# Scaling decoded weights by rms_g: GpSimd's multiplication given to ScalarE in a fused attention and MLP kernel

## The chip, the cores and the metric

The kernel runs on one core of a Trainium2 chip. The metric is the device time of one execution in microseconds. The core's engines are TensorE (PE in the profile: matmuls; PEld: their weight loads), VectorE (DVE), ScalarE (ACT), GpSimd (POOL) and SyncE (SP, which issues the DMAs). Each engine takes its instructions in the order in which the code issues them; a semaphore makes an instruction wait for one of another engine.

## What is computed

Linear attention with random features, then a gated MLP with RMS normalization, then a second MLP. Inputs are 64-bit floats. After the attention, x has 2304 tokens and 512 features:

```python
def _moe_ref(x, w_gate, w_val, w_out, rms_g):       # d_ff = 1536
    rms = np.sqrt(np.mean(x * x, axis=-1, keepdims=True) + 1e-06)
    xn = x / rms * rms_g
    g = xn @ w_gate
    silu = g * (1.0 / (1.0 + np.exp(-g)))
    val = xn @ w_val
    return (silu * val @ w_out).astype(np.float32)

def _moe2_ref(x, w_in, w_out):                      # d_ff = 2048
    h = x @ w_in
    g = h * (1.0 / (1.0 + np.exp(-h)))
    return (g @ w_out).astype(np.float32)
```

The factor rms_g belongs to a row of w_gate and of w_val, so the kernel multiplies the weights by it and leaves x alone.

## The kernel before

**Precision.** Every product of the two MLPs is made from split operands: a high part (a copy rounded to fp32r) and a low part (value minus high part), in three matmuls (PASS: high by high, high by low, low by high).

**Tokens and sweeps.** The tokens lie in five blocks j: four of 512 tokens and block 4 of 256. The hidden columns lie in groups f of 128; five sweeps cover the 12 groups of the gated MLP (2, 3, 2, 3, 2 groups) and six sweeps the 16 of the second. A sweep goes over all blocks. For each group of a block in the gated MLP (g1_glu), TensorE makes the gate product (12 matmuls, PSUM tile "ps_g", of which there are four), ScalarE takes its SiLU (line 259), TensorE makes the value product, VectorE multiplies both (line 265), ScalarE copies the high part of the result (line 235) and VectorE subtracts the low part (line 236). The product with w_out of the whole block, here called the second product (g2_glu, line 296), is held back: it is issued behind the first gate product of the next block, and in block 4 behind the first pair of products. VectorE adds its four tiles ("ps_y", four too) into ya (line 307); in the first sweep ScalarE copies them (line 305).

**Weights.** A weight block is a job: a gate (g), value (v) or w_out (o) block, named below with its group, as v4 or o4. The jobs go through a pipeline with one stage per tick:

- load: a DMA of 512 KB into raw;
- decode (w_decode): five steps on VectorE (lines 156 to 167), two integer additions on GpSimd (line 170), and for g and v blocks a multiplication by rms_g on GpSimd (line 173). All write one tile m, of which there are two;
- w_high: ScalarE copies the high part (line 186);
- w_low, called w_lo here: VectorE subtracts the low part (line 189), which reads m too.

In one tick the oldest job comes first: w_low of one, w_high of the next, decode of a third, load of a fourth. stream() yields the cost of each product just ahead of issuing it (and of each second-product tile just behind it); the loop at the end of the kernel adds these costs and calls a tick where they pass 3.2 us (while the weights of the second sweep are not all there) or 5.5 us. A product whose weights are missing (prep.need) calls ticks too. The place of a tick's instructions in each engine's order follows from these sums alone.

**The first phase** (to about 200 us) holds the attention and the first sweep of blocks 0 to 2. A planner (run_order) orders it; there add_weight issues the same steps for 9 jobs, seven of them g or v blocks (four of the first sweep, then g2, v2 and g3), with w_decode's step 7 for the multiplication. The other 17 g and v blocks (v3, g4, v4, then g5 to v6, g7 to v9, g10 to v11) go through the ticks.

Of the kernel before, what the change touches and what calls it, by code (L numbers as in the profile page):

```python
# [8 lines left out]
F32 = mybir.dt.float32  # L9
# [4 lines left out]
AF = mybir.ActivationFunctionType  # L14
# [6 lines left out]
def kernel(  # L21
# [14 lines left out]
    nc = tc.nc  # L36
# [7 lines left out]
    KC = DM // P  # L44
    TB = 4
    EDGE, SHIFT = 72, 16
    scale = 1.0 / float(D) ** 0.25
# [42 lines left out]
    g_sb = const.tile([P, KC], F32)  # L90
# [17 lines left out]
    f = 0  # L108
# [4 lines left out]
    f = 0  # L113
# [26 lines left out]
    def w_load(job, st, n):  # L140
        raw = rawp.tile([P, KC, P, 2], U32, tag=f"raw{n}", name=f"raw{n}", bufs=1)
        ap = job[3]
        if len(ap.shape) == 2:
            nc.sync.dma_start(out=raw.rearrange("p c f w -> p (c f w)"), in_=ap)
        else:
            nc.sync.dma_start(out=raw.rearrange("p c f w -> p c (f w)"), in_=ap)
        words = raw.rearrange("p c f w -> p (c f) w")
        st.low, st.high = words[:, :, 0], words[:, :, 1]


    def w_decode(job, st, step, n=None):
        ts, tt = nc.vector.tensor_scalar, nc.gpsimd.tensor_tensor
        low, high = st.low, st.high
        if step == 0:
            st.m = rawp.tile([P, KC * P], U32, tag=f"m{n}", name=f"m{n}", bufs=1)
            ts(out=st.m, in0=high, scalar1=1, scalar2=1,  # L156
               op0=ALU.logical_shift_left, op1=ALU.logical_shift_right)
        elif step == 1:
            ts(out=low, in0=low, scalar1=2.0 ** -29, scalar2=None, op0=ALU.mult)
        elif step == 2:  # L160
            mf = st.m.bitcast(F32)
            ts(out=mf, in0=mf, scalar1=EXP_LO, scalar2=EXP_HI, op0=ALU.max, op1=ALU.min)
        elif step == 3:
            ts(out=high, in0=high, scalar1=0x80000000, scalar2=0x40000000,
               op0=ALU.bitwise_and, op1=ALU.bitwise_or)
        elif step == 4:
            ts(out=st.m, in0=st.m, scalar1=3, scalar2=None, op0=ALU.logical_shift_left)
        elif step < 7:
            mi = st.m.bitcast(I32)
            tt(out=mi, in0=mi, in1=(low if step == 5 else high).bitcast(I32), op=ALU.add)  # L170
        else:
            mf = st.m.bitcast(F32).rearrange("p (c f) -> p c f", c=KC)
            tt(out=mf, in0=mf, in1=g_sb.rearrange("p (c o) -> p c o", o=1).to_broadcast([P, KC, P]), op=ALU.mult)

    def scaled(job):
        return job[2][1] in "gv"

# [16 lines left out]
    class Prep:  # L194
# [13 lines left out]
        def tick(self):  # L208
            for e in self.pipe:
                job, st, n, step = e  # L210
                if step == 0:
                    for s in range(8 if scaled(job) else 7):
                        w_decode(job, st, s, n)
                else:
                    (w_high if step == 1 else w_low)(job, st)
                e[3] += 1
            self.pipe = [e for e in self.pipe if e[3] < 3]
            if self.jobs:
                self.n ^= 1
                e = [self.jobs.pop(0), State(), self.n, 0]  # L220
                w_load(e[0], e[1], self.n)
                self.pipe.append(e)
# [679 lines left out]
    def add_weight(job, n, gate):  # L902
        st = State()
        pr = W_PRIO + n

        def load(o):
            w_load(job, st, o.slot["raw"])

        lop = Op("ld_w", "SP", 2.0, load, gate, pr, ["raw"])
        prev = head = None  # L910
        for s in range(5):
            prev = Op(
                "w_dec", "DVE", 0.37, lambda o, s=s: w_decode(job, st, s, o.slot.get("wm")), [lop, prev], pr,
                [] if s else ["wm"], port=True,
            )
            head = head or prev
        for s in (5, 6, 7) if scaled(job) else (5, 6):
            prev = Op(
                "w_add", "Pool", 1.38, lambda o, s=s: w_decode(job, st, s), [prev, g_op], pr,
                free=[(lop, "raw")] if s == 6 else [],  # L920
            )
        hi = Op("w_hi", "ACT", 0.54, lambda o: w_high(job, st), [prev], pr)
        w_done[job[2]] = Op("w_lo", "DVE", 0.61, lambda o: w_low(job, st), [hi], pr, free=[(head, "wm")], port=True)
# [98 lines left out]
    with tc.manual_schedule():  # L1022
# [16 lines left out]
        def split_omega(e, c):  # L1039
# [3 lines left out]
            else:  # L1043
# [8 lines left out]
                out=om, in_=omega.rearrange("m (o d) -> m o d", o=1).to_broadcast([P, 2, D])  # L1052
# [67 lines left out]
```

## Time and profile before

| | |
|---|---|
| median of 3 runs | 998.92 us (998.87 to 999.29) |
| the profiled execution | 998.12 us, span from first to last instruction 996.0 us |
| granted TensorE clock, mean | 0.999 |
| busy: PE, DVE, ACT, POOL | 979.2, 575.9, 381.0, 312.7 us |
| multiplications by rms_g on GpSimd | 24, from 46.5 to 451.6 us |

A row of the timeline gives start and duration in us, engine, line, operation, the tile written and the tiles read, sizes, and a count where neighbours are merged. Square brackets hold the time the engine stood idle just before and what ended it. An engine that is seldom busy can still be in the way, if another waits for it at the wrong time; so the places where TensorE is not busy are looked for first, and then what ended them.

### The profile page before, as it was taken

To read this page: it belongs to the slowest core of one execution; us is meant where nothing else is said; L and a number is where in the kernel's file an instruction comes from. 1 tells how busy PE (TensorE), PEld (TensorE's weight loads), DVE (VectorE), ACT (ScalarE), POOL (GpSimd) and SP (SyncE) were. 2 spreads that over 40 slices of the span, in tenths; PEclk is the share of its full clock that TensorE was granted. 3 is DMA by queue.
4 is the path that set the end of the run, shared out by engine and by line. 5 is a ranking of instruction groups with operands and counts; after the bars stand their busy time and mean duration, and the time that the engine had idled before them with its cause. 6 is when DMAs were issued, how large, how long until landed. Compare 5 with 4: busy or idle time off the path is not lost.

```text
span 996.0 us, 15344 instructions
## 1 busy us (share of the span) xinstructions
PE 979.2 (98%) x5999; PEld 835.1 (84%) x5999; DVE 575.9 (58%) x1167; ACT 381.0 (38%) x855; POOL 312.7 (31%) x325
## 2 busy tenths in 40 slices
PE   7998999999999999999999999999999999999998
PEld 6988998888788888888888888888888888888887
DVE  6999998358843346685234683623644644525633
ACT  5999996543221112212112334442322322222321
POOL 7877764236610025453000332312312312201200
PEclk9999999999999999999999999999999999999999
DMA  7554312003210002222000220110200211100023
GB/s 197 148 128 108 106 45 64 22 23 105 85 43 1 1 22 64 80 80 74 1 1 1 64 64 23 62 43 22 85 22 22 68 39 27 59 1 22 21 85 106
DMA packets 69112, 55.58 MB, mean 56 GB/s; under 512 B 26160, under 2 KB 63280, under 8 KB 69040
## 3 DMA queue, kind: packets, MB, share of 16 engines
q1 hardware_dynamic: 69040, 54.60, 18.4%
q8 instruction: 47, 0.77, 0.3%
q14 instruction: 25, 0.20, 0.1%
HBM read 49.87 MB, written 4.72 MB: 55 GB/s over the span
## 4 chain that ended last, share of the span: by engine, by line
PE 89%; DVE 5%; ACT 3%; issue 1%; DMA 0%; SPq 0%; DVEq 0%; ACTq 0%
PE g L242 44%; PE y L329 20%; PE y L296 12%; PE b L626 4%; PE b L242 3%; PE b L999 2%; ACT e L668 2%; PE kv L694 1%; PE b L752 1%; PE b L777 1%; DVE small L643 1%; PE b L605 1%; DVE w L189 1%; PE b L878 1%; DVE m L156 1%
## 5 line engine op out<-in xcount | busy, mean ns | idle before, releaser
L242 PE MATMUL g<-xs,w 128*128 128x512 f32 (+1 forms) x2256 | 468.0, 366 | 0.0
L242 PEld LDWEIGHTS g<-xs,w 128*128 128x128 f32 x2256 | 391.1, 188 | 70.0
L170 POOL TENSOR_TENSOR m<-m,raw 128x512 int32<-128x512 int32 x136 | 190.5, 1401 | 562.3 <-issue 421.4
L236 DVE TENSOR_TENSOR h<-s,h 128x512 fp32r<-128x512 f32 (+1 forms) x134 | 96.9, 724 | 185.1 <-ACT h L235 185.1
L329 PE MATMUL y<-w,h 128*128 128x512 f32 (+1 forms) x870 | 200.8, 388 | 0.0
L329 PEld LDWEIGHTS y<-w,h 128*128 128x128 f32 x870 | 162.2, 188 | 33.2
L235 ACT ACTIVATE h<-s 128x512 fp32r<-128x512 f32 (+1 forms) x134 | 78.7, 588 | 183.3 <-DVE s L265 161.3
L296 PE MATMUL y<-h,w 128*128 128x512 f32 (+1 forms) x648 | 136.0, 366 | 1.3 <-DVE w L189 1.2
L296 PEld LDWEIGHTS y<-h,w 128*128 128x128 f32 x648 | 112.0, 189 | 22.0 <-DVE w L189 1.8
L276 ACT ACTIVATE s<-g 128x512 f32<-128x512 f32 (+1 forms) x80 | 44.4, 556 | 171.0 <-PE g L242 170.9
L340 DVE TENSOR_TENSOR ya<-y,ya 128x512 f32<-128x512 f32 (+1 forms) x91 | 62.1, 684 | 57.9 <-PE y L329 56.6
L186 ACT ACTIVATE w<-m 128x512 fp32r<-128x512 f32 x68 | 42.9, 631 | 116.4 <-POOL m L170 69.0
L307 DVE TENSOR_TENSOR ya<-y,ya 128x512 f32<-128x512 f32 (+1 forms) x80 | 50.1, 634 | 53.5 <-PE y L296 53.3
L668 ACT ACTIVATE e<-b,nb 128x128 f32<-128x128 f32 x272 | 78.5, 418 | 4.7 <-DVE nb L656 4.0
L265 DVE TENSOR_TENSOR s<-s,g 128x512 f32<-128x512 f32 (+1 forms) x54 | 33.8, 626 | 76.8 <-PE g L242 75.1
L626 PE MATMUL b<-bd,hl 128*128 128x256 f32 x432 | 65.2, 295 | 2.8 <-DVE hl L614 1.8
L626 PEld LDWEIGHTS b<-bd,hl 128*128 128x128 f32 x432 | 56.3, 193 | 5.9 <-DVE hl L614 2.5
L189 DVE TENSOR_TENSOR w<-m,w 128x512 fp32r<-128x512 f32 x68 | 55.6, 817 | 0.2 <-ACT w L186 0.2
L643 DVE TENSOR_REDUCE small<-b 128x4 f32<-128x512 f32 x72 | 50.0, 695 | 5.2 <-PE b L626 2.5
L259 ACT ACTIVATE s<-g 128x512 f32<-128x512 f32 (+1 forms) x54 | 29.5, 547 | 59.2 <-PE g L242 59.1
L558 POOL TENSOR_TENSOR sq<-sq 128x256 f32<-128x256 f32 (+2 forms) x80 | 45.0, 579 | 1.9
L554 POOL TENSOR_TENSOR sq<-x 128x512 f32<-128x512 f32 (+1 forms) x40 | 39.0, 982 | 19.1 <-DVE small L649 9.9
(69 smaller groups left out, 737.8 us busy)
## 6 DMA issues: line engine op xcount, KB each, us to landing
raw<-in_moe_w_out_dram SPq DMA_DIRECT2D x28, 512.0 KB, 3.5
raw<-in_moe_w_in_dram SPq DMA_DIRECT2D x16, 512.0 KB, 3.6
raw<-in_moe_w_gate_dram SPq DMA_DIRECT2D x12, 512.0 KB, 3.6
raw<-in_moe_w_val_dram SPq DMA_DIRECT2D x12, 512.0 KB, 3.5
x<-in_k_dram SPq DMA_DIRECT2D x16, 256.0 KB, 3.2
va<-in_v_dram SPq DMA_DIRECT2D x32, 128.0 KB, 3.2
x<-in_q_dram SPq DMA_DIRECT2D x16, 256.0 KB, 2.9
out_dram<-ya SPq DMA_DIRECT2D x15, 256.0 KB, 2.0
```

The costliest lines, as they stand in the source:

```text
L170: tt(out=mi, in0=mi, in1=(low if step == 5 else high).bitcast(I32), op=ALU.add)
L189: nc.vector.tensor_tensor(out=st.t[:, 1, :], in0=st.m.bitcast(F32), in1=st.t[:, 0, :].bitcast(F32), op=ALU.subtract)
L235: nc.scalar.activation(out=ht[:, 0, :], in_=s, func=AF.Copy)
L236: nc.vector.tensor_tensor(out=ht[:, 1, :], in0=s, in1=ht[:, 0, :].bitcast(F32), op=ALU.subtract)
L242: nc.tensor.matmul(out=ps, lhsT=w[:, a, cc * P:(cc + 1) * P], rhs=xs[j][:, c, cc, :], start=(n == 0), stop=(n == 3 * KC - 1),)
L296: nc.tensor.matmul(out=ps, lhsT=wt[1, "o", f][:, a, d * P:(d + 1) * P], rhs=hs[f][:, c, :], start=(n == 0), stop=(n == nn - 1),)
L307: nc.vector.tensor_tensor(out=y[:, d, :], in0=ps, in1=y[:, d, :], op=ALU.add)
L329: nc.tensor.matmul(out=ps, lhsT=hs[f][:, a, t * P:(t + 1) * P], rhs=wt[2, "p", f][:, c, d0:d1], start=(n == 0), stop=(n == nn - 1),)
L340: nc.vector.tensor_tensor(out=o[:, t, d0:d1], in0=ps, in1=o[:, t, d0:d1], op=ALU.add)
L626: nc.tensor.matmul(out=st.ps[r][:, 2 * j:2 * j + 2, :].rearrange("p h m -> p (h m)"), lhsT=st.hl[:, c, 2 * r + j, :], rhs=bd[:, a, :], sta ...
L643: nc.vector.tensor_reduce(out=st.mx[:, G * r:G * r + G], in_=st.ps[r], axis=AX.X, op=ALU.max)
L668: nc.scalar.activation(out=st.e[r][:, h, :], in_=st.ps[r][:, h, :], func=AF.Exp, bias=st.nb[:, G * r + h:G * r + h + 1],)
```

## The change

In the ticks the decode stage now issues steps 0 to 6 only. For g and v blocks it then issues w_scale: four ScalarE operations, each of which multiplies 128 columns of m in place (the 128 rows of the weight block that share one column of g_sb) by an operand per partition. They stand in ScalarE's order behind w_high of the job before and ahead of whatever the stream issues next. The first phase is left as it was.

```diff
+    def w_scale(st):
+        mf = st.m.bitcast(F32).rearrange("p (c f) -> p c f", c=KC)
+        for c in range(KC):
+            nc.scalar.activation(out=mf[:, c], in_=mf[:, c], func=AF.Copy, scale=g_sb[:, c:c + 1])
...
             for e in self.pipe:
                 job, st, n, step = e
                 if step == 0:
-                    for s in range(8 if scaled(job) else 7):
+                    for s in range(7):
                         w_decode(job, st, s, n)
+                    if scaled(job):
+                        w_scale(st)
                 else:
                     (w_high if step == 1 else w_low)(job, st)
```

## Rows read from the trace of the kernel before

**Rows 1.** The page, part 1: busy us, share of the span, instructions.
```profile
PE 979.2 (98%) x5999; PEld 835.1 (84%) x5999; DVE 575.9 (58%) x1167; ACT 381.0 (38%) x855; POOL 312.7 (31%) x325
```

**Rows 2.** Windows: busy us of each engine in two stretches of 50 us.
```profile
200.00:250.00 50.00, 49.03 (x251) 41.20 (x249) 35.80 (x56) 19.49 (x36) 23.88 (x18) 1.00 0.20 64
...
300.00:350.00 50.00, 50.00 (x274) 43.52 (x273) 15.16 (x26) 7.33 (x14) 0.00 (x0) 1.00 0.00 1
```

**Rows 3.** The chain that ended last: start, us, engine, tile, line, count.
```profile
212.24 1.68 issue
...
248.53 1.78 DVE w L189
250.35 6.64 PE y L296 x28
...
354.21 5.44 PE y L296 x24
```

**Rows 4.** Three lines by themselves: ns of one (min/median/max), first and last start.
```profile
L173 POOL TENSOR_TENSOR m<-m,g_sb x24: 1036/1077/1470, 46.5 to 451.6; 128x512 f32<-128x512 f32 x24
...
L668 ACT ACTIVATE e<-b,nb x272: 359/403/567, 14.2 to 160.3; 128x128 f32<-128x128 f32 x136
...
L189 DVE TENSOR_TENSOR w<-m,w x68: 678/684/1804, 63.4 to 946.6; 128x512 fp32r<-128x512 f32 x68
```

**Rows 5.** Timeline from 212 to 229 us.
```profile
212.31 2.70 POOL L170 TENSOR_TENSOR m<-m,raw 128x512 int32<-128x512 int32 x2 [12.48 <-DVE m L167]
...
217.66 0.43 DVE L236 TENSOR_TENSOR h<-s,h 128x256 fp32r<-128x256 f32 x1 [0.48 <-ACT h L235]
...
223.19 1.26 DVE L162 TENSOR_SCALAR m<-m 128x512 f32<-128x512 f32 x1
...
224.71 0.42 DVE L167 TENSOR_SCALAR m<-m 128x512 uint32<-128x512 uint32 x1
224.74 0.37 ACT L259 ACTIVATE s<-g 128x256 f32<-128x256 f32 x1
...
226.04 0.80 DVE L236 TENSOR_TENSOR h<-s,h 128x256 fp32r<-128x256 f32 x1 [0.49 <-ACT h L235]
...
227.56 3.04 PE L296 MATMUL y<-h,w 128*128 128x256 f32 x24
...
228.59 1.15 DVE L156 TENSOR_SCALAR m<-raw 128x512 uint32<-128x512 uint32 x1
```

**Rows 6.** Timeline of ScalarE in the first phase.
```profile
143.55 1.14 ACT L668 ACTIVATE e<-b,nb 128x128 f32<-128x128 f32 x4
144.55 0.41 ACT L610 ACTIVATE hl<-b 128x256 fp32r<-128x256 f32 x1
```

**Rows 7.** Timeline from 362 to 368 us, around weight g7.
```profile
362.19 2.69 POOL L170 TENSOR_TENSOR m<-m,raw 128x512 int32<-128x512 int32 x2 [80.88 <-issue]
...
367.92 0.69 DVE L265 TENSOR_TENSOR s<-s,g 128x512 f32<-128x512 f32 x1 [2.50 <-PE g L242]
```

**Rows 8.** Timeline from 246 to 248 us, around weight g5.
```profile
246.19 0.42 DVE L167 TENSOR_SCALAR m<-m 128x512 uint32<-128x512 uint32 x1
...
247.23 0.63 ACT L235 ACTIVATE h<-s 128x512 fp32r<-128x512 f32 x1 [2.31 <-DVE s L265]
```

**Rows 9.** Timeline from 403 to 415 us, around weight v9.
```profile
403.27 0.43 DVE L156 TENSOR_SCALAR m<-raw 128x512 uint32<-128x512 uint32 x1
...
404.62 0.42 DVE L167 TENSOR_SCALAR m<-m 128x512 uint32<-128x512 uint32 x1
...
406.69 1.87 DVE L307 TENSOR_TENSOR ya<-y,ya 128x512 f32<-128x512 f32 x3
...
412.70 0.91 DVE L236 TENSOR_TENSOR h<-s,h 128x256 fp32r<-128x256 f32 x1 [0.48 <-ACT h L235]
...
414.18 3.04 PE L296 MATMUL y<-h,w 128*128 128x256 f32 x24
```

**Rows 10.** Timeline from 430 to 442 us, around weight g10.
```profile
430.48 2.69 POOL L170 TENSOR_TENSOR m<-m,raw 128x512 int32<-128x512 int32 x2 [3.09 <-issue]
...
433.40 8.46 PE L296 MATMUL y<-h,w 128*128 128x512 f32 x36
```

## The prediction

> **What bounds the kernel now.** First the busy times: TensorE is busy for 98% of the span, no other engine for more than 58% [rows 1]. Then the stretches, for where its idle time lies: 0.97 us of 50 between 200 and 250 us, none between 300 and 350 [rows 2]. So behind the first phase there is next to nothing to win, and what makes TensorE wait shows in full. Then the chain that ended last: it leaves TensorE for VectorE between 212 and 250 us, where the low halves of the decoded weights are written, and comes back at 250.35, when VectorE's w_lo of block 4 of w_out lets a product go on; from there it is TensorE alone, 24 matmuls of 512 columns in 5.44 us [rows 3], 0.227 each, and half of that for the 256 columns of token block 4. The stretch to 250 is the one place where VectorE's order counts.
>
> **What goes.** 17 of the 24 multiplications on GpSimd [rows 4]; seven weights are prepared in the first phase and keep it. At some 1.1 us that is 19 us of an engine that is busy 31% [rows 1]. Nobody on TensorE's path waits for it, save by way of VectorE, whose operations lose time beside GpSimd's: a decode step of 0.42 took 1.26 where a multiplication ran, another 1.15 [rows 5].
>
> **What comes.** 17 times four ScalarE operations, no DMA and no queue of DMAs moved. Their own price is not in the trace. The nearest are the four exponentials of 128 columns, with an operand per row as here: the next operation started 1.00 us after the first [rows 6]. Above, four of their median duration of 0.403 [rows 4] with no overlap are 1.6 us; below 1.00 nothing speaks for a gain, as ScalarE did none of this. I take 1.1, close to the like shape. By the Trainium skill (ScalarE: Activation LUTs, What ACT_TABLE_LOAD costs) such an operation takes about 0.39 us and overlaps the next by 0.09: an estimate of 1.17 for four, 0.4 us more in the sum below. The row is shorter than that.
>
> **What moves is a wait.** Before, ScalarE met a weight first in w_high, one tick after the decode. Now it stands at the first scaling until VectorE's five steps and GpSimd's two additions (2.70 us [rows 5]) of the same tick are done. Queued behind it is whatever the code issues next. Walking through the yields of the stream and adding their amounts, behind the 17 stand: the high copy of an activation 8 times, a SiLU 4, the next w_high 4, a copy out of PSUM once. Behind a held SiLU or high copy, VectorE in turn stands at the product or the low half. TensorE has four PSUM tiles to run ahead with, so it stops only where the low half of a block's last column group comes too late for the second product; that follows one first product later.
>
> Where it is hidden: for g7 the additions end at 364.88, the scaling at 366.0, so high copy and low half end by 367.4, ahead of VectorE's next product at 367.92 [rows 7]. Nothing lost, and g8, g9, v7, v8 go like it: their lateness is below 0.7 us, with a whole first product to make it good. If that cover went, each would cost about what the next cases do. Three places are not hidden.
>
> (A) Weight v4, next in ScalarE's queue the SiLU of the 256-column block. v3 first: its additions end at 215.01, so the high copy behind it starts at 216.15. That copy (0.63 as in [rows 8]), its low half (0.7), and product, copy and low half of the following short block (1.3) bring VectorE to 218.8, where it was at 218.09 [rows 5]. g4's scaling only holds back copies out of PSUM whose tiles nobody wants yet. This 0.7 comes back, since a step of v4's decode no longer lies beside a multiplication (1.26 against 0.42): the decode ends at 225.1 as before. Additions to 227.85, scaling to 228.95. SiLU to low half took 1.30 to its start, and 0.43 where nothing disturbed it [rows 5]: done at 230.7. The second product starts at 227.56 and wants that low half four matmuls of 0.113 later, at 228.0. **TensorE waits 2.7.**
>
> (B) The same for VectorE: its low half ends at 230.7 instead of 226.84, 3.9 late. Its next w_lo then meets no GpSimd (0.68, the median of [rows 4], where there were 1.75 up to the step at 228.59; less 1.1), and that step no multiplication (0.42 instead of 1.15; less 0.7) [rows 5]: 2.1 late. VectorE is full to 250, so that stays. g5's decode, ended at 246.61 [rows 8], ends at 248.7; additions 251.5; scaling 252.6; then the high copy of block 4, which ran from 247.23 [rows 8], to 253.3, its low half 0.7 to 254.0, w_lo 0.7 to 254.7. TensorE went on at 250.30 behind that w_lo [rows 3]. **The delay is now 4.4, A included.** The three weights after it (v5, g6, v6) hold ScalarE too, but behind them stands a second product of 8 us that needs nothing of it; by the same steps v6 lets ScalarE go at about 270, and the next second product starts at about 277.
>
> (C) Weight v9, again with the short block's SiLU behind it. Its decode ended at 405.04 [rows 9]; lateness from g9 adds 0.2. Additions to 408.05, scaling to 409.15, SiLU to low half to 410.9. Behind these on VectorE stand four additions into ya (0.62 each, to 413.4), a w_lo (0.7 [rows 4]) and the decode of the next weight (1.77 from first start to last end), to 415.7, and then the product, the copy and the low half of the second column group, this last beside GpSimd (0.91 [rows 9]): 417.5. The second product started at 414.18 [rows 9] and wants it at 414.6. **2.9 lost.**
>
> (D) Weight g10, with the high copy of block 9 behind it. Additions end at 433.17, scaling 434.3, high copy 434.9, low half 435.65, w_lo 436.3. The second product starts at 433.40 [rows 10] and wants the last of these after 8 matmuls, at 435.2. **1.1 lost.**
>
> Sum: 4.4 + 2.9 + 1.1 = 8.4. The profiled execution took 998.12, its span 996.0; this becomes 1006.5. The median of the runs is 998.92, 0.8 above the profiled one, so the forecast is 1007.3.
>
> Bounds. The scaling enters A twice (v3 and v4), B once more, C twice, D once. At 1.0 the sum is 0.6 less, at 1.6 it is 3 more: 1010.3. If v3's lateness does not come through (0.7 in A), C's low half finds GpSimd quiet (0.5) and D is hidden (1.1), the forecast is 1005.0; with the lower price 1004.4.
>
> **Rivals.** *The cover holds.* The low halves come in time, ScalarE's wait is slack everywhere, and the time stays at about 998.9. For it: ScalarE is busy for 19.49 of 50 us there [rows 2], and g7 shows the cover. Against: at v4 the second product wants the low half at 228.0, 1.2 us after it was done [rows 5], and the hold of ScalarE, from 225 to 229, is longer. That is the point that decides: holds that delay a low half by less than 1.2 us cost nothing. It is the outcome on the other side.
>
> *VectorE freed.* Between 212 and 228 a multiplication cost VectorE about 0.8 and 0.7 us [rows 5], and TensorE waited for VectorE at 250. If only that counted, the 0.97 of idle up to 250 [rows 2] and the 0.35 from there to 250.35 [rows 3] would go: 997.6 at best, which is still within 0.2%. The Trainium skill says why such operations suffer (SBUF — State Buffer, SBUF: two separate sides): GpSimd and VectorE take a shared port by turns, each for a whole instruction. The trace agrees: w_lo has a median of 0.684 and a maximum of 1.804 [rows 4]. Against it as the outcome: the hold of ScalarE is longer than what VectorE gains.
>
> *Not what it says.* Were the scalings put next to w_high in the queue, nobody would wait, and the time is 998.9. But the rows of before stand in the order in which the code issues them.
>
> *Part of it.* B's chain finds slack or C's second column group passes early: A by itself (2.7) up to A with C (5.6), 1001.6 to 1004.5.
>
> *More.* The scalings run one after another because they read and write the same tile, with a gap each: 2.4 for four, 8 more in the sum, 1011 to 1015.
>
> **How the numbers follow.** Forecast 0.70; cover holds 0.05; VectorE freed 0.03; not what it says 0.02; part of it 0.10; more 0.10. Range 1004.0 to 1011.5, which leaves out the rivals; with edges of *more* and *part of it* that fall inside it holds near 0.8. This kernel's time can be told from no change beyond about 0.2%, 2.0 us. Faster by that much needs more idle time of TensorE than there is: 0.02. Within it: cover, VectorE freed and misplacement, less that 0.02: 0.08. Slower: 0.90.
>
> **What would show it.** GpSimd: 7 multiplications left, 68 ScalarE operations at the new line. ScalarE's longest waits are for GpSimd's additions at that line. TensorE waits for low halves at three places: about 2.7 near 228, near 255 some 1.7 more than the kernel before had at 250, some 3 near 420, 1 near 443. Wrong if TensorE idles at other second products (then the cover of g7 to v8 or of v6 was misjudged), or if the four scalings are far from 1.1.

## The result and the profile after

The changed kernel takes 1008.92 us (median of 4 runs, 1007.35 to 1009.31), the kernel before 998.89 (4 runs). The ratio is 1.0099, with a 95% interval of 1.0084 to 1.0114: 10.0 us slower, where 8.4 were forecast. The profiled execution took 1007.35 us with a span of 1005.5, 9.2 and 9.5 above those of before.

The page of the changed kernel, parts 1 and 5 (its lines from 174 on stand 5 lower, from 217 on 7 lower: line 296 is now 303, 242 is 249, 235 and 236 are 242 and 243, 189 is 194; the scaling is line 178):

```profile
PE 982.6 (98%) x5999; PEld 836.0 (83%) x5999; DVE 561.6 (56%) x1167; ACT 400.3 (40%) x923; POOL 290.8 (29%) x308
...
L303 PE MATMUL y<-h,w 128*128 128x512 f32 (+1 forms) x648 | 139.6, 370 | 7.4 <-ACT h L242 6.1
...
L178 ACT ACTIVATE m<-m,g_sb 128x128 f32<-128x128 f32 x68 | 21.8, 391 | 74.1 <-POOL m L170 74.1
```

Beside [rows 1], GpSimd lost 17 operations and 22 us, VectorE 14 us with the same number of operations, and ScalarE gained 68 operations and 19 us. None of that is near a limit. What counts is idle time: 7.4 us of TensorE ahead of the second product (1.3 before), mostly for ScalarE's high copy of an activation, and 74.1 us of ScalarE ahead of the scaling, for GpSimd's additions. The view of waits gives the same pairs (total us, times, longest):

```profile
ACT m L178 <- POOL m L170: 74.1, 17, 10.0
...
PE y L303 <- ACT h L242: 6.1, 3, 2.2
PE y L303 <- DVE h L243: 1.0, 3, 0.5
```

Seventeen holds of ScalarE, and four places where TensorE runs dry. The idle times in brackets add up to less than the loss, so losses are taken below from the start of one product to the start of a later one. The first place, the timeline from 224 to 231 us, to be read against [rows 5]:

```profile
224.43 0.41 DVE L167 TENSOR_SCALAR m<-m 128x512 uint32<-128x512 uint32 x1
...
224.98 2.69 POOL L170 TENSOR_TENSOR m<-m,raw 128x512 int32<-128x512 int32 x2 [1.43 <-ACT m L178]
...
227.70 1.28 ACT L178 ACTIVATE m<-m,g_sb 128x128 f32<-128x128 f32 x4 [0.87 <-POOL m L170]
227.72 0.51 PE L303 MATMUL y<-h,w 128*128 128x256 f32 x3
228.89 0.36 ACT L266 ACTIVATE s<-g 128x256 f32<-128x256 f32 x1
229.28 0.42 DVE L272 TENSOR_TENSOR s<-s,g 128x256 f32<-128x256 f32 x1 [4.44 <-ACT s L266]
...
230.18 0.43 DVE L243 TENSOR_TENSOR h<-s,h 128x256 fp32r<-128x256 f32 x1 [0.48 <-ACT h L242]
230.20 3.11 PE L303 MATMUL y<-h,w 128*128 128x256 f32 x21 [1.97 <-ACT h L242]
```

The SiLU of the short block, at 224.74 before, starts at 228.89, right behind the four scalings. VectorE stands 4.44 us for it. TensorE does three matmuls of the second product at 227.72 and then stands until the high copy is there. The second place, from 248 to 262 us; first TensorE in the kernel before (see also [rows 8]), then the changed kernel:

```profile
250.35 6.64 PE L296 MATMUL y<-h,w 128*128 128x512 f32 x28 [1.20 <-DVE w L189]
256.83 5.38 PE L242 MATMUL g<-xs,w 128*128 128x512 f32 x23
```

```profile
248.12 0.42 DVE L167 TENSOR_SCALAR m<-m 128x512 uint32<-128x512 uint32 x1
...
248.67 2.67 POOL L170 TENSOR_TENSOR m<-m,raw 128x512 int32<-128x512 int32 x2 [2.48 <-issue]
...
251.38 1.28 ACT L178 ACTIVATE m<-m,g_sb 128x128 f32<-128x128 f32 x4 [4.53 <-POOL m L170]
252.56 0.61 ACT L242 ACTIVATE h<-s 128x512 fp32r<-128x512 f32 x1
...
253.23 0.49 PE L303 MATMUL y<-h,w 128*128 128x512 f32 x1 [2.21 <-ACT h L242]
...
253.82 0.68 DVE L194 TENSOR_TENSOR w<-m,w 128x512 fp32r<-128x512 f32 x1
253.96 8.46 PE L303 MATMUL y<-h,w 128*128 128x512 f32 x29 [0.23 <-DVE h L243]
...
262.26 13.08 PE L249 MATMUL g<-xs,w 128*128 128x512 f32 x57
```

w_lo ends at 254.50, 4.2 us behind the 250.30 of before. But the 29 matmuls from 253.96 on take 8.46 us, where 28 took 6.64 before. The windows say why. A row has the length of the window, the busy us and the instructions of PE, PEld, DVE, ACT and POOL, and at its end the granted clock as a share of full speed, the DMA share and GB/s:

```profile
250.00:252.00 2.00, 1.02 (x5) 0.52 (x3) 0.00 (x0) 0.62 (x3) 1.29 (x1) 1.00 0.00 0
252.00:254.00 2.00, 0.54 (x2) 0.23 (x2) 0.79 (x2) 2.00 (x6) 0.00 (x0) 0.94 0.77 214
254.00:256.00 2.00, 2.00 (x4) 1.41 (x5) 1.97 (x6) 0.18 (x1) 0.00 (x0) 0.50 0.17 57
256.00:258.00 2.00, 2.00 (x8) 1.63 (x7) 0.91 (x2) 0.00 (x0) 1.48 (x2) 0.71 0.00 0
258.00:260.00 2.00, 2.00 (x11) 1.63 (x10) 1.60 (x3) 0.84 (x3) 1.12 (x1) 1.00 0.00 0
```

TensorE comes out of a stretch in which it did one matmul (251.02 to 253.96), and its granted clock is at the lower of its two levels (1.2 instead of 2.4 GHz) for some 3 us. By the gate product that follows, 262.26 against 256.83 before, the delay is 5.4: 4.2 of waiting and 1.2 of clock. The kernel before had a shorter wait at this spot, 1.20 us, and kept 1.00.

The third place, at a later short block, and the fourth, 20 us behind it, beside [rows 9] and [rows 10]; again first the kernel before, then the changed one:

```profile
408.60 5.75 PE L242 MATMUL g<-xs,w 128*128 128x256 f32 x36
...
417.06 16.51 PE L242 MATMUL g<-xs,w 128*128 128x512 f32 x72
...
441.69 16.48 PE L242 MATMUL g<-xs,w 128*128 128x512 f32 x72
```

```profile
413.48 1.28 ACT L178 ACTIVATE m<-m,g_sb 128x128 f32<-128x128 f32 x4 [5.46 <-POOL m L170]
414.02 5.75 PE L249 MATMUL g<-xs,w 128*128 128x256 f32 x36
...
422.00 0.89 DVE L243 TENSOR_TENSOR h<-s,h 128x256 fp32r<-128x256 f32 x1 [0.48 <-ACT h L242]
422.02 0.38 PE L303 MATMUL y<-h,w 128*128 128x256 f32 x1 [1.90 <-ACT h L242]
422.94 2.65 PE L303 MATMUL y<-h,w 128*128 128x256 f32 x20 [0.54 <-DVE h L243]
425.43 16.51 PE L249 MATMUL g<-xs,w 128*128 128x512 f32 x72
...
441.57 1.28 ACT L178 ACTIVATE m<-m,g_sb 128x128 f32<-128x128 f32 x4 [3.86 <-POOL m L170]
...
444.02 0.68 DVE L194 TENSOR_TENSOR w<-m,w 128x512 fp32r<-128x512 f32 x1
444.16 7.25 PE L303 MATMUL y<-h,w 128*128 128x512 f32 x29 [0.23 <-DVE h L243]
451.24 9.00 PE L249 MATMUL g<-xs,w 128*128 128x512 f32 x39
```

From the start of the products at 414.02 to those at 425.43 the changed kernel needs 11.41 us, the kernel before 8.46 (408.60 to 417.06): 2.95 lost. To the next at 451.24 it is 25.81 against 24.63: 1.18 lost. In all 4.2 + 1.2 + 2.95 + 1.18 = 9.5, the difference of the spans. From 265 to 400 and from 450 to 980 both kernels keep TensorE busy without a gap.

### The profile page after: what moved, and what is told of

Read it like the earlier page. It is cut to its first block, busy times and chain, and to the rows that moved or that the text cites. A ratio compares the mean times of both kernels' runs of the same rounds, so it can differ in the third digit from the quotient of the medians.

```text
span 1005.5 us, 15400 instructions
## 1 busy us (share of the span) xinstructions
PE 982.6 (98%) x5999; PEld 836.0 (83%) x5999; DVE 561.6 (56%) x1167; ACT 400.3 (40%) x923; POOL 290.8 (29%) x308
## 4 chain that ended last, share of the span: by engine, by line
PE 55%; ACT 0%; DVE 0%; issue 0%
PE g L249 30%; PE y L336 20%; PE y L303 6%; ACT m L178 0%; DVE w L194 0%; ACT h L242 0%; DVE ya L347 0%; DVE h L243 0%
## 5 line engine op out<-in xcount | busy, mean ns | idle before, releaser
L170 POOL TENSOR_TENSOR m<-m,raw 128x512 int32<-128x512 int32 x136 | 187.9, 1382 | 595.2 <-issue 444.3
L243 DVE TENSOR_TENSOR h<-s,h 128x512 fp32r<-128x512 f32 (+1 forms) x134 | 92.5, 691 | 209.2 <-ACT h L242 209.2
L303 PE MATMUL y<-h,w 128*128 128x512 f32 (+1 forms) x648 | 139.6, 370 | 7.4 <-ACT h L242 6.1
L194 DVE TENSOR_TENSOR w<-m,w 128x512 fp32r<-128x512 f32 x68 | 53.4, 786 | 0.2 <-ACT w L191 0.2
L178 ACT ACTIVATE m<-m,g_sb 128x128 f32<-128x128 f32 x68 | 21.8, 391 | 74.1 <-POOL m L170 74.1
```

What stands on the lines that cost most here:

```text
L194: nc.vector.tensor_tensor(out=st.t[:, 1, :], in0=st.m.bitcast(F32), in1=st.t[:, 0, :].bitcast(F32), op=ALU.subtract)
L243: nc.vector.tensor_tensor(out=ht[:, 1, :], in0=s, in1=ht[:, 0, :].bitcast(F32), op=ALU.subtract)
L303: nc.tensor.matmul(out=ps, lhsT=wt[1, "o", f][:, a, d * P:(d + 1) * P], rhs=hs[f][:, c, :], start=(n == 0), stop=(n == nn - 1),)
```

## The experiments

The theory: ScalarE is held, in its order of instructions, until GpSimd's additions of the same tick are done; what stands behind the hold makes low halves late for four second products. The rival: 68 more ScalarE operations, 20 us of its time, have a price of their own, spread over all weights. Each run has the kernel before beside it, whose median moved between 998.1 and 998.9; the ratios are to those runs. The expectations reckon from the 998.9 of the kernel before; where it ran faster beside them, the differences count. The diffs are against the changed kernel.

**The same scalings, one tick later.** They stand right ahead of the weight's high copy, where ScalarE waited for GpSimd already in the kernel before.

```diff
                 if step == 0:
                     for s in range(7):
                         w_decode(job, st, s, n)
-                    if scaled(job):
-                        w_scale(st)
                 else:
+                    if step == 1 and scaled(job):
+                        w_scale(st)
                     (w_high if step == 1 else w_low)(job, st)
```

> The same 68 ScalarE scalings, each four now issued one tick later, right ahead of the weight's own high copy, where ScalarE used to wait anyway. Theory (ScalarE held too early, so that low halves come late for the second product): nobody is held, TensorE waits nowhere for a high copy, and the time is that of the kernel before or up to 1.3 us less, 997.6 to 999.2. Rival (the price of 68 more ScalarE operations, some 20 us of its time): the price is all there, so 1006 to 1009.

Measured: 996.9 us (11 runs, 996.3 to 997.76), ratio 0.9984 (0.9975 to 0.9993). It has the 68 operations and no loss: it is faster than the kernel before, by 0.16%. That is below the range of the theory too, which allowed 1.3 us less; 1.7 came. The page says what ScalarE does, the waits what it waits for now, and the timeline shows the spot near 250:

```profile
PE 980.0 (98%) x5999; PEld 836.4 (84%) x5999; DVE 567.0 (57%) x1167; ACT 402.3 (40%) x923; POOL 292.3 (29%) x308
...
ACT m L178 <- POOL m L170: 24.2, 9, 3.7
...
250.46 6.65 PE L303 MATMUL y<-h,w 128*128 128x512 f32 x28 [0.57 <-DVE w L194]
```

ScalarE is as busy as in the changed kernel (402.3 and 400.3 us), but waits for the additions 24.2 us instead of 74.1, and TensorE's one wait behind the first phase is 0.57, less than the 1.2 of before. The rival falls here. Of the 1.7 us, 1.0 was won at this spot (9.03 us from the second product at 247.91 to the gate product at 256.94, in the kernel before 10.05 from 246.78 to 256.83). Some 0.3 lies outside the span from first to last instruction: time less span is 1.8 in each of its runs and 2.1 to 2.2 in each of the kernel before, and no run shows why.

**The hold without the operations.** GpSimd multiplies as before; only the high copy of the 17 weights is issued in the tick of the decode.

```diff
                 if step == 0:
-                    for s in range(7):
+                    for s in range(8 if scaled(job) else 7):
                         w_decode(job, st, s, n)
                     if scaled(job):
-                        w_scale(st)
-                else:
-                    (w_high if step == 1 else w_low)(job, st)
+                        w_high(job, st)
+                elif step == 2:
+                    w_low(job, st)
+                elif not scaled(job):
+                    w_high(job, st)
```

> No ScalarE scaling at all: GpSimd multiplies as before, but the high copy of the 17 weights is issued in the tick of the decode, so that ScalarE stands there for the additions and the multiplication. Theory: the hold is as long as in the changed kernel or longer (1.1 of multiplication and 0.5 of copy against 1.2 of scaling, and VectorE's steps stay slow beside the multiplication): as much lost or more, 1008 to 1014. Rival (price of the new operations): there are none, so 998.9.

Measured: 1015.18 us (4 runs, 1014.76 to 1016.65), ratio 1.0170 (1.0156 to 1.0184), 1.2 above the upper end. No new operation, and a larger loss than that of the change: the place in the order is enough. The waits ahead of second products (in this kernel line 305, the high copy line 244, the low half line 245), and a window:

```profile
PE y L305 <- ACT h L244: 8.5, 6, 3.3
PE y L305 <- DVE h L245: 1.5, 6, 0.3
...
234.00:236.00 2.00, 2.00 (x11) 2.00 (x11) 2.00 (x6) 0.77 (x2) 0.17 (x1) 0.50 0.00 0
```

TensorE waits at six second products for a high copy, where the changed kernel did at three, and the waits for low halves come on top: ten us in all. In two stretches of 8 us each, from 232 and from 426, the windows of 2 us show a granted clock of 0.50 to 0.80. The clock was not in what was expected, and the time lies above its upper end.

**Thirteen of seventeen.** The changed kernel, with v4, g5, v9 and g10 multiplied on GpSimd.

```diff
-                    for s in range(7):
+                    early = job[2][1:] not in (("v", 4), ("g", 5), ("v", 9), ("g", 10))
+                    for s in range(8 if scaled(job) and not early else 7):
                         w_decode(job, st, s, n)
-                    if scaled(job):
+                    if scaled(job) and early:
                         w_scale(st)
```

> The changed kernel with four weights (v4, g5, v9, g10) given back to GpSimd's multiplication; the other 13 are scaled on ScalarE at once, and hold it. Theory: the 13 holds are covered by the four PSUM tiles and by the first product, and cost 0 to 0.6 us (v3 delays a low half by 0.3): 998.7 to 999.6. Rival (price of the operations): 13 of 17 of the loss, 1006 to 1007.

Measured: 998.54 us (10 runs, 998.28 to 999.05), ratio 1.0002 (0.9993 to 1.0012). On balance the thirteen holds cost nothing that can be measured; the four that were named carry the loss. The trace (second product at line 304) is less clean. Near 228, where v4 is back on GpSimd, TensorE still waits for a low half:

```profile
229.84 2.66 PE L304 MATMUL y<-h,w 128*128 128x256 f32 x20 [0.67 <-DVE h L244]
```

The scaling of g4 ends at 225.5 there; behind it the copies out of PSUM that it held back and a w_high run until 227.5, and only then the SiLU of the short block. The wait near 250 is 0.81 and not 1.20 in return. From the second product at 217.07 to the gate product at 257.96 it is 40.89 us, in the kernel before 40.34 (216.49 to 256.83): 0.55 more, within the 0 to 0.6 expected.

**One weight at a time.** The kernel before, with a single weight scaled on ScalarE at once (the condition above turned into `job[2][1:] == ("v", 4)` and so on).

> The kernel before with one weight alone, v4, scaled on ScalarE at once. Theory: the short block's SiLU is held, its second product waits some 3.0 us near 228; VectorE is 2.3 behind up to 250, so the wait there shrinks by 0.7: 2.3 in all, 1001.2 (1000.5 to 1001.9). Rival (a price spread over all 68 operations): a seventeenth of 9, 999.4.

Measured: 1001.25 us (10 runs, 999.62 to 1001.68), ratio 1.0028 (1.0019 to 1.0038).

> The kernel before with g5 alone scaled on ScalarE at once. Theory: the high copy of block 4 is held until 250.6, w_lo of o4 ends at 252.65 and not 250.30: 2.35 more, 1001.3 (1000.6 to 1001.9), and up to 1.7 more if TensorE's granted clock falls behind the wait near 250 as in the changed kernel. Rival (price): 999.4.

Measured: 1002.38 us (5 runs, 1001.26 to 1002.53), ratio 1.0036 (1.0023 to 1.0049).

> The kernel before with v9 alone scaled on ScalarE at once. Theory: the second product of the short block waits near 414 as in the changed kernel, 2.7 (without the 0.2 that g9 adds): 1001.6 (1000.9 to 1002.2). Rival (price): 999.4.

Measured: 1001.59 us (6 runs, 1001.09 to 1001.89), ratio 1.0032 (1.0020 to 1.0045).

> The kernel before with g10 alone scaled on ScalarE at once. Theory: the second product waits for w_lo of o9 near 435: 1.1 to 1.2 more, 1000.0 (999.6 to 1000.4). Rival (price): 999.4. The four single weights should add up to about 8.4, with the clock's share beside it.

Measured: 999.21 us (10 runs, 998.72 to 999.79), ratio 1.0010 (1.0000 to 1.0019). It lies below the theory's 999.6 and near the rival's 999.4, but the kernel before ran at 998.1 beside it: by the ratio it is 1.0 more, where the theory had 1.1 to 1.2 and the rival 0.5, and the interval holds both. Its trace decides: from the second product at 433.49 to the gate product at 442.96 it is 9.47 us, in the kernel before 8.29 (433.40 to 441.69), so 1.18 is lost at this one place. The other three are far from the rival.

The ratios give 2.8, 3.6, 3.2 and 1.0 us (forecast 2.3, 2.35 and up to 1.7 more, 2.7, 1.1 to 1.2), 10.6 in all; the whole change costs 10.0. For three of them the timeline of TensorE splits the loss (line 250 is the gate or value product, 304 the second product, 243 the high copy). v4 alone, then g5 alone, then v9 alone:

```profile
230.10 3.12 PE L304 MATMUL y<-h,w 128*128 128x256 f32 x21 [2.41 <-ACT h L243]
233.06 16.51 PE L250 MATMUL g<-xs,w 128*128 128x512 f32 x72
...
252.20 6.64 PE L304 MATMUL y<-h,w 128*128 128x512 f32 x28 [0.82 <-DVE w L194]
258.68 5.60 PE L250 MATMUL g<-xs,w 128*128 128x512 f32 x24
```

```profile
246.74 1.52 PE L304 MATMUL y<-h,w 128*128 128x512 f32 x6
251.24 10.31 PE L304 MATMUL y<-h,w 128*128 128x512 f32 x30 [2.98 <-ACT h L243]
261.39 2.88 PE L250 MATMUL g<-xs,w 128*128 128x512 f32 x12
```

```profile
413.69 0.51 PE L304 MATMUL y<-h,w 128*128 128x256 f32 x3
415.94 0.39 PE L304 MATMUL y<-h,w 128*128 128x256 f32 x1 [1.73 <-ACT h L243]
416.86 4.15 PE L304 MATMUL y<-h,w 128*128 128x256 f32 x20 [0.54 <-DVE h L244]
420.85 16.51 PE L250 MATMUL g<-xs,w 128*128 128x512 f32 x72
```

v4: from the second product (227.18) to the next products 5.88 us, before 2.87 (227.56 to 230.43), so 3.0 lost; at 250 the wait for w_lo has shrunk from 1.2 to 0.82, and up to the gate product at 258.68 it is 31.50, before 29.27: 2.2 lost, as expected. g5: from 246.74 to 261.39 it is 14.65, before 10.05, so 4.6 lost. w_lo ends at 252.50, 2.2 later (2.35 were worked out); the 28 matmuls behind it take 8.8 us, before 6.5, and that 2.3 is the clock, 0.50 to 0.69 in the windows from 250 to 258. v9: 7.16 against 2.88, 4.3 lost, with 20 matmuls in 4.15 where the changed kernel's took 2.65: 1.5 of it is the clock (0.50 from 418 to 420).

**A shorter scaling.** Only the first of the four operations.

```diff
-        for c in range(KC):
+        for c in range(1):
             nc.scalar.activation(out=mf[:, c], in_=mf[:, c], func=AF.Copy, scale=g_sb[:, c:c + 1])
```

> The changed kernel with only the first of the four scalings of each weight, so three quarters of rms_g are left out; the wait for GpSimd stays. Theory: the hold stays and is 0.9 us shorter at each weight. By the steps of the prediction: 1.2 near 228, 2.0 in all by 255, 1.9 near 420, 0.3 near 443: 4.2 more than before, 1003.1 (1002 to 1004.5), with a shorter wait near 253 and so perhaps none of the low clock there. Rival (price): a quarter of the loss, 1001 to 1001.5. If the length of the scaling did not matter: 1008 to 1009.

Measured: 1002.1 us (4 runs, 1001.68 to 1002.57), ratio 1.0036 (1.0023 to 1.0050), 3.6 more; in the profiled execution the span is 4.1 above that of before, as the sum of 4.2 wanted, and the mean granted clock is 1.000. So the length of the scaling enters several times over, as the bounds had it: 0.9 us less at a weight takes 5.4 us off the span, 1.2 of them clock. The rival's 1001 to 1001.5 is not far off, so this run by itself would not have told the two apart.

**No multiplication at all** for the 17 weights.

```diff
-                    if scaled(job):
-                        w_scale(st)
```

> The 17 weights are multiplied by rms_g on no engine (the factor is left out of them). Neither GpSimd's multiplication nor ScalarE's operations are there: what remains is the best that taking the multiplication off can give. Theory: TensorE's work sets the time and its idle time near 250 was all there was to win, so the ratio to the kernel before is that of the kernel that scales one tick later (0.9984), within 0.9975 to 0.9993. Rival (68 ScalarE operations have a price even where nobody waits): clearly below it, 0.996 or less.

Measured: 996.56 us (11 runs, 996.05 to 997.63), ratio 0.9982 (0.9973 to 0.9991). That is the ratio of the kernel that scales one tick later within its interval: where nobody waits for them, the 68 operations cost nothing that can be measured, and 1.8 us is all that taking the multiplication off GpSimd can bring. In its trace 1.2 of that lies at the spot near 250 (8.83 us from 246.68 to 255.51), and the 0.3 outside the span is there again.

## Why the prediction was right, step by step

**What bounds the kernel**: right. TensorE's waits show in full. The most that was there to win is 1.8 us (forecast 1.3); of that 1.2 is the idle time that the forecast meant, and 0.3 lies outside the span.

**What moves**: right. In the trace the operations behind the 17 scalings are 8 high copies, 4 SiLUs, 4 w_high and the copies out of PSUM once, as counted.

**The price of four scalings**: 1.1 was taken; 227.70 to 228.89 is 1.19 from the first to the operation behind them, 0.387 us for one by itself. The exponentials had given 1.00. The Trainium skill's figures (ScalarE: Activation LUTs, What ACT_TABLE_LOAD costs) gave 0.39 and an estimate of 1.17, and the trace agrees with these better than with the row that was used. In the sum it made no difference, by luck: GpSimd's additions and VectorE's decode came 0.2 us sooner than worked out at A and B.

**A, the short block behind v4**: decode end 224.84 (forecast 225.1), additions 227.67 (227.85), SiLU 228.89 (228.95), low half 230.61 (230.7). The 2.7 is 2.7 by the next products, 233.16 against 230.43, but made up of other parts: 2.57 at the second product (5.44 us from 227.72 to 233.16, before 2.87), 0.33 at the one before it (24 matmuls in 5.97 us, 5.64 before), which v3's hold cost and which had been put at nothing, less 0.17 by which this trace enters the stretch sooner (202.49 against 202.66). That v3's 0.7 comes back in v4's decode was right.

**B, VectorE's lateness and g5**: decode end 248.54 (248.7), additions 251.34 (251.5), high copy from 252.56 (252.6), w_lo 254.50 (254.7). The delay of 4.4 is 4.2. Beside it the step lacked the clock, 1.2 here.

**C and D**: 2.9 forecast, 2.95 found; 1.1 and 1.18.

**What is hidden**: v3 and g4 apart, the run with thirteen weights shows it, and the holds of v5, g6 and v6 in the changed kernel go by without a gap of TensorE. That nobody wants what g4's scaling holds back was wrong with v4 on GpSimd, where it made a SiLU late; in the changed kernel v4's own hold hides it.

**The rivals**: the cover does not hold at four weights; the freed VectorE is real, but shows only where nobody is held (0.9984). The one on the place in the order was the right thing to ask: by the ratios that place is worth 11.5 us.

**The sum**: the waits are 4.2 + 2.95 + 1.18 = 8.3, where 8.4 were worked out. The forecast is still 1.6 below the median. One term was left out, TensorE's clock: behind waits of this length it can run at its lower level for some us, and then each wait costs more than its length. In the profiled execution that was 1.2 us at one place. The rest is open: the other three runs were 1.2 to 2.0 us longer than the profiled one, where 0.8 had been allowed, with mean granted clocks of 0.996 and 0.997 instead of 0.998. More places with a low clock would fit that, but no trace of theirs shows one, and the mean clock does not order the times (1008.60 at 0.996, 1009.31 at 0.997).

## What to carry to other kernels

Giving an operation to an idle engine also gives that engine's queue a new waiting place: look at what stands behind it in program order and who waits for that, and put it where the engine waits for the same thing already; here that moved the same 68 operations from 10 us lost to 1.6 us won. Count a stall by the last thing the consumer needs (here the low half of the last column group), and not by the length of the hold: the longest idle time of ScalarE, 10.0 us ahead of g7's scaling, cost nothing, and the shortest, 0.87 ahead of v4's, came with 2.6 us lost at the second product behind it. When a wait of TensorE is added, add to its price what its clock may cost behind it (here 0 to 2.3 us).

## What the hardware showed that was not expected

The granted clock fell behind some waits and not behind others of much the same length. In the changed kernel it was 0.50 behind the wait that ended at 253.2 (2.21 us), and 1.00 behind those near 228 and 420 (1.97, and 1.90 with 0.54). With v9 alone it fell to 0.50 behind 1.73 and 0.54 at the place where the changed kernel kept it; with v4 alone the profiled execution kept it behind 2.41. That execution is also the fastest of its ten runs (999.62 us at a mean clock of 1.000); the other nine show 0.997 or 0.998 and took 999.81 to 1001.68. What decides it is open. Its price where it fell: 1.2 us in the changed kernel, 1.5 with v9 alone, 2.3 with g5 alone. Nor does the mean clock account for the whole time: with v9 alone the four runs at 1.000 took 1001.09 to 1001.62, the two at 0.998 1001.69 and 1001.89.
